# Linear attention and a gated FFN in one kernel: another written-out order, four output buffers, fewer matmuls on zeros

## The chip, the cores and the metric

The kernel runs on one core of a Trainium2 chip. The metric is the device time of one execution in microseconds. Before the change its median is 379.44 us over three runs (379.32 to 381.07).

## What is computed

Attention with an exponential feature map (batch 8, 8 heads, 576 tokens, head width 64, 128 features), then a gated FFN over the 4608 tokens of width 512:

```python
def phi(x):
    proj = np.einsum('bhsd,df->bhsf', x, w_phi)
    proj = proj - np.max(np.abs(proj), axis=-1, keepdims=True)
    return np.concatenate([np.exp(proj), np.exp(-proj)], axis=-1)
q_p, k_p = (phi(q), phi(k))
kv = np.einsum('bhsf,bhsd->bhfd', k_p, v)
z = np.sum(k_p, axis=2)
num = np.einsum('bhsf,bhfd->bhsd', q_p, kv)
den = np.einsum('bhsf,bhf->bhs', q_p, z)[..., None] + 1e-06
x = (num / den) ...                      # 4608 x 512
gate = np.maximum(x @ w_gate, 0.0)       # 512 -> 1536
return (gate * (x @ w_val)) @ w_out      # 1536 -> 512, float32
```

Everything is drawn and returned in float32; the kernel multiplies in bfloat16.

## The kernel before

The kernel is cut into 1430 small steps ("atoms", `Atoms`, L91), each a Python closure that issues a few instructions. The string ORDER lists their numbers; `Atoms.run` (L106) calls them in that order, and nothing else sets the order of the instructions on any engine. A number with an apostrophe calls the step's other variant: a PSUM copy goes to the other engine (ACT or DVE), a product of POOL to DVE. A word `zN` calls `keep_busy` (L196), which issues matmuls on a tile of zeros, two to a matmul of 128 x 512 and a single one as 128 x 256; their result is never read. Each engine works through its own instructions in the order in which they were issued, and waits at one whose inputs or buffers aren't ready.

The steps of one batch of keys ("items" of 4 to 8 blocks of 128 rows; `K_CUTS` cuts batch 0 into items of 4, 4, 8, 8, 8 and 4 blocks):

- load k and v. For batches 0 and 1, PE turns the blocks (L266) and DVE or ACT copies them out of PSUM (tile tT, L279); later batches are turned by a DMA on SP's queue (L291).
- project with w_phi (64-row matmuls, L307) into two PSUM banks; DVE takes the largest absolute value per row (tile mk, L314); ACT takes two exponentials per bank (tile kp, L363), and then the exponentials of the row maxima (tile ek, L374).
- scale v by them (tile vs, L323 on POOL; in the other variant a small ACT copy, L388, and DVE).
- 72 matmuls per half batch give kv (L447); ACT or DVE copies it (tile kv, L401).

For queries, in two pairs of chunks of 128 tokens per batch: turn (tile tT8 for batches 0 and 1), project both ways (L485 for the exponentials, L307 for the row maxima), two exponentials per bank on ACT (tile qp, L503), maxima on DVE (tile mq), their exponential on ACT (tile cq, L519); then matmuls with kv (L533), a product and a sum on DVE for each of three groups of heads (L552, L564), a reciprocal (L571) and the division on POOL (tile xu, L573), and the turn into xT (on PE for batches 0 and 1, L593; by DMA later).

The FFN (`ffn`, L652) runs in nine groups of 512 tokens: one per batch and a ninth for the batches' last 64 tokens each. A group has 12 value steps and 12 gate steps of four 128-row matmuls (L661); group 0 has 16, since its first 8 are only 256 tokens wide (`FIRST`). The value's copy goes to ACT or DVE (tile val_sb, L676), the gate's product is always DVE's (tile h, L683). Four output tiles of 12 matmuls follow (L709), each copied by ACT or DVE (L723) into an output buffer and stored by SP's queue. PSUM has eight banks, one pool for all.

The weights come in three thirds of w_val and w_gate and one load of w_out, all issued by POOL (L241, L250) between its other work, at the place that ORDER gives them. The transposing loads, the v loads and the stores are issued by SP, in their order too.

Of the kernel before, what the change touches and what calls it, by code (L numbers as in the profile page):

```python
# [8 lines left out]
FP32 = mybir.dt.float32  # L9
BF16 = mybir.dt.bfloat16  # L10
# [12 lines left out]

ORDER = """7 z6 49 50 59 60' z1 61 65 8 64 51 0 69 70' z1 71 1 62 66 67 68 z4 79 52 54 53 56 89 57 63 72 74 73
55 76 58 80 90 77 78 75 81 85 82 83 84 86 88 99 100' 91 92 94 z5 115 93 116 154 155 95 87 118 101
102 105 120 122 96 103 104 123 109 111' 124 128 10 127 126 110' 117 223 98 125 106 163 224 119 167
203 121 157 130 159 2 204 129 131 156 158 160 165 142 143 144 132 97 107 108 112 113' 4 114 161 193
z1 136 137 194' 29 45 133 134 162 166 138 135 148 149 3 139 145 146 9 150 147 151 233 168 187 181  # L30
184 185 182 188 164 234' 186 189 183 249 250' 190 205 140 141' 169 170 213 214' 152 153 175 209 176
288 289 207 172 173 177 174 171 178 1095 1096 1097 1098 1099 1100 208 1101 191 192' 179 180 195 199
1102 1103 196 13 206 235 237 198 239 1104 1105 1106 1107 1108 5 200 236 1109 1110 197 238 215 225
227 216 11 218 6 240 242 226 241 1111 1112 228 217 220 221 1113 252 291 254 256 293 1114 230 231'
219 1115 1116 210 229 1117 295 297 301 296 300 232 222 246 299 33 328 330 251 253 255 332 211 1118
247 248' 1119' 1120 201 298 258 290 292 262 202 260 294 212 243 257 244 245' 327 261 1121 1122 263
276 277 279 278 280 333 282 283 284 281 285 1123 1124 1125 309 302 310 329 303 304 1126 1127 318
319 320 259 321 322 306 307 1128 267 323 311 331 315 316 317 34 1129 1130 308 305 268 312 269 286
287 345 347 348 349 324 361 353 357 12 346 350 354 14 1131 1132' 355 363 264 1133 356 325 270 16
271 364 272 1134 326' 313 314' 1135 1136 265 266 273 362 366 367 365 358 360 337 338 339 1137 369  # L40
373 377 381 274 275 378 1138 370 371 372 374 380 351 379 1139' 1140 35 1141 352 391 395 36 359 433
437 375 397 435 1142 401 1143 399 368 340 341 334 342 1144 30 46 1145' 1146 393 1147 335 336 382
383 398 426 430 428 400 1148 1149 402 1150 384 432 434 376 17 427 431 429 436 385 387' 392 386 388
438 394 396 403 389 390' 461 463 477 480 19 1151 1152 410 481 411 462 1153 464 412 1154 1155 478 37
# [3 lines left out]
1168' 517 1169 485 488 486 495 474 548 552 508 512 497 468 510 490 498 499' 487 483 1170 18 1171'  # L48
550 1172 492' 1173 489 1174' 500 1175 1176 1177 1178 1179' 507 509 549 553 475 38 511 551 484 491
# [4 lines left out]
1198 676 678 680 603 606 627 1199 628 558 630 604 559 631 608 555 556 557 617' 632 602 541 629 1200  # L54
1201 1202 584 583 605 560 564 565 590 591 592 1203 1204 1205 1206 607 585 586 642 646 644 711 715
619 622 1207 587 588 589 623 620 593 624 626 712 714 713 1208 1209 21 1210 609 621 1211' 1212 1213'
1214 41 648 650 652 633 594 40 647 31 641 643 651 1215' 1216 1217' 649 1218 1219' 1220 645 682 686
610 684 677 634 679 635 637' 636 681 625 638 639 683 687 640 653 685 727 731 665 728 666 1221 1222
729 667 1223 730 657 658 659 688 47 716 26 1224 654 655 656 668 669 660 661 662 670 1225 1226 1227
717 671 672 673 1228 695 696 697 1229' 743 747 744 746 663 757 745 719 674 723 1230 720 1231 721  # L60
722 664 1232 703 704 1233' 1234 759 692 693 25 724 725 700 675 24 1235 726 689 732 705 701 718 702
748 1236 734' 694 706 707 708 690 691 698 1237 1238 793 795 799 761 797 798 699 800 733' 801 1239
802 1240 1241 735 739 709 758 710 737 762 760 764 766 749 738 736 740 768 750 344 769 803 1242 1243
1244 1245 1246' 792 796 828 741 832 804 830 751 794 827 753 742 754 755' 42 752 763 767 1247' 1248
756 787 788 781 782 789 765 833 783 43 32 1249' 1250 822 823 824 48 1251' 784 785 829 776 786 831
27 1252 777 790 1253 1254 773 774 845 846 775 861 863 791 847 778 1255 864 862 1256 1257' 770 771
865 849 772 779 808 809 1258 1259 840 810 1260 1261 819 841 842 1262 866 848 837 838 839 1263 1264
1265 1266 820 816 817 811 850 852 821 812 1267 1268 818 825 805 806 1269 1270 1271 853 813 807 780
867 897 899 855 856 869 870 872 1272 1273' 826 814 815 874 875 1274 1275 834 901 851 873 857 835
836 1276' 1277 1278 871 854 858 892 896 894 876 961 965 962 859 860 877 1279' 879 880 963 881 878  # L70
882 884 843 883' 1280 1281 1282 927 891 895 931 964 893 1283 929 1284 1285' 1286 1287' 932 934 898
900 936 902 903 1288 1289' 926 930 933 928 935 937 868 888 890 889 885 887 969 971 993 994 938 886'
977 970 996 995 979 1290 1291' 1292 1293 997 972 973 978 974 1294 1295' 981 921 922 923 1296 1297'
910 911 907 908 909 980 912 1298 1299 28 44 1300 1301 918 919 920 915 916 917 904 985 988 976 987
924 925 1007 1302 1303 986 1009 998 999 1304 1000 1011 950 951 982 983 905 906 844 953 1305' 1306
954 956 957 958 942 943 955 952 959 944 1307 1308 1309' 984 939 960 940 945 989 913 914 1310 1311
946 947 1014 1016 966 967 1018 1042 1046 941 948 990 1043 1047 1312 1313 949 1314 1315' 1045 1044
1316 1317 1318' 1013 1015 1017 1049 1051 968 975 1001 1002' 1003 991 992 1004 1005' 1006' 1048 1050
1008 1012 1319 1053 1054 1010 1019 1031 1032 1320 1321 1058 1322 1323' 1324 1033 1023 1325' 1052
1020 1069 1070 1326 1327 1061 1062 1063 1059 1060 1071 1328 1072 1329' 1037 1330 1073 1055 1056  # L80
1038 1039 1331 1332 1333 1334 1034 1035 1036 1021 1057 1064 1040 1024 1074 1335' 1336 1337 1338
1066 1067 1068 1339' 1340 1341 1342 1343 1026 1077 1079 1041 1065 1022 1078 1082 1075 1076 1344
1027 1028 1025 1029 1030 1081 1345' 1346 1347 1084 1080 1348 1349 1090 1350 1351' 1352 1083 1091
1087 1088 1092 1085 1086 1353 1354' 1355' 1356 1357' 1089 1358 1359' 1360 1361 1362 1363 1364 1365'
1366 1367' 1093 1094 1368 1369 1370 1371' 1372 1373' 1374 1375' 1376 1377 1378 1379 1380 1381' 1382
1383 1384 1385 1386 1387 1388 1389 1390 1391' 1392 1393' 1394 1395 1396 1397 1398 1399 1400 1401'
1402 1403 1404 1405' 1406 1407' 1408 1409 1410 1411' 1412 1413' 1414 1415 1416 1417' 1418 1419 1420
1421 1422 1423' 1424 1425 1426 1427 1428 1429'"""


class Atoms:  # L91
# [28 lines left out]
def kernel(  # L120
# [24 lines left out]
    DM = out.shape[1]  # L145
    P = 128
# [502 lines left out]
            q_tails(b // 2)  # L649


    def ffn(g):  # L652
        st = {}
        steps = [(fi, 0, SF) for fi in range(NFC)]
# [42 lines left out]

        for t in range(4):
            cols = LAST if g == B and t == 3 else ((0, DM),)
            for part, (c0, c1) in enumerate(cols):  # L700
                for third in range(3):

                    @atoms.add("fo", g, t, part, third)
                    def _(alt, t=t, part=part, third=third, c0=c0, c1=c1):
# [18 lines left out]
                        copy_by(copy_of(alt, "ACT", "DVE"))(out_sb, po)  # L723
                        store(t, out_sb, c0, c1)
# [55 lines left out]
```

## Time and profile before

| | us |
|---|---|
| median of three runs | 379.44 |
| the profiled execution | 381.42 |
| its span, first to last instruction | 379.6 |
| PE busy in the span | 368.2 |
| DVE busy | 288.1 |
| ACT busy | 218.0 |
| POOL busy | 136.2 |

A busy time is the union of an engine's instructions. The durations below come from the profiled execution, so sums are made against its 381.42 us, which is 2.0 us above the median.

### The profile page before, as it was taken

How to read it: one execution, taken by the hardware profiler on the slowest of the kernel's cores; microseconds unless marked ns; L12 is line 12 of the kernel's file. 1: busy time of each engine (PE TensorE's matmuls, PEld its weight loads, DVE VectorE, ACT ScalarE, POOL GpSimd, SP SyncE). 2: the span in 40 equal slices, each digit the busy share in tenths (PEclk: the TensorE clock that was granted, in tenths of full speed). 3: DMA queues.
4: the chain of work that ended last, by engine and by line, in shares of the span. 5: the costliest groups of instructions: out<-in, count | busy, mean ns of one | idle time of the engine just before them, and what ended most of it. 6: DMA issues, size and time to landing. Idle time of an engine off the chain costs nothing.

```text
span 379.6 us, 9748 instructions
## 1 busy us (share of the span) xinstructions
PE 368.2 (97%) x3891; PEld 196.7 (52%) x3891; DVE 288.1 (76%) x638; ACT 218.0 (57%) x538; POOL 136.2 (36%) x188
## 2 busy tenths in 40 slices
PE   6879999999999999999999999999999999999996
PEld 3557655546545555465555544545465454444443
DVE  2888988888986897889978987799677848723641
ACT  4978996988577867684776649766261221012101
POOL 5867451774247135441761137213810220100000
PEclk9989999999999999999999999999999999999999
DMA  8999997997969619793789503631400130011003
GB/s 254 205 195 195 208 173 92 241 226 103 153 202 240 119 29 166 218 172 52 138 225 149 152 2 111 98 46 28 120 36 2 29 112 28 16 51 59 2 2 109
DMA packets 75356, 45.15 MB, mean 119 GB/s; under 512 B 49392, under 2 KB 66352, under 8 KB 75312
## 3 DMA queue, kind: packets, MB, share of 16 engines
q1 hardware_dynamic: 53872, 30.42, 33.9%
q0 software_dynamic: 20960, 13.57, 26.2%
q8 instruction: 30, 0.49, 0.6%
q10 hardware_dynamic: 480, 0.56, 0.5%
q14 instruction: 14, 0.11, 0.1%
HBM read 37.78 MB, written 9.44 MB: 124 GB/s over the span
## 4 chain that ended last, share of the span: by engine, by line
PE 92%; ACT 6%; DMA 1%; issue 0%; SPq 0%; DVE 0%; DVEq 0%
PE pa L661 49%; PE pa L709 25%; PE pa L533 5%; PE pa L447 5%; PE pa L307 4%; ACT kp L363 3%; PE pa L485 2%; ACT qp L503 2%; PE pa L266 1%; DMA vn<-in_k_dram 1%; ACT tT L279 1%; ACT ek L374 0%; ACT xT L593 0%; SPq L218 0%; DVE u L723 0%
## 5 line engine op out<-in xcount | busy, mean ns | idle before, releaser
L661 PE MATMUL pa<-xT,wg_sb 128*128 128x512 bf16 (+1 forms) x400 | 99.3, 371 | 0.6 <-ACT val_sb L676 0.6
L709 PE MATMUL pa<-wo_sb,h 128*128 128x512 bf16 (+2 forms) x444 | 99.3, 373 | 0.0
L661 PE MATMUL pa<-xT,wv_sb 128*128 128x512 bf16 (+1 forms) x400 | 99.3, 370 | 0.0
L683 DVE SCALAR_TENSOR_TENSOR h<-pa,val_sb 128x512 bf16<-128x512 f32 (+1 forms) x112 | 74.5, 668 | 29.2 <-PE pa L661 21.8
L503 ACT ACTIVATE qp<-pa 128x512 bf16<-128x512 f32 x144 | 76.0, 613 | 25.2 <-PE pa L485 22.3
L573 POOL TENSOR_TENSOR xu<-u,r 128x512 bf16<-128x512 f32 x36 | 37.3, 1042 | 143.1 <-DVE r L571 111.3
L676 ACT CAST val_sb<-pa 128x512 bf16<-128x512 f32 (+1 forms) x70 | 39.7, 570 | 82.8 <-PE pa L661 78.1
L323 POOL TENSOR_TENSOR vs<-vn,ek 128x512 bf16<-128x512 f32 (+1 forms) x75 | 69.9, 945 | 41.9 <-ACT ek L374 33.5
L363 ACT ACTIVATE kp<-pa 128x512 bf16<-128x512 f32 (+1 forms) x164 | 79.0, 570 | 8.1 <-PE pa L307 6.9
L661 PEld LDWEIGHTS <-wv_sb 128*128 128x128 bf16 x448 | 41.7, 98 | 44.9 <-issue 1.1
L661 PEld LDWEIGHTS <-wg_sb 128*128 128x128 bf16 x448 | 41.4, 98 | 45.2 <-issue 1.5
L709 PEld LDWEIGHTS <-h 128*128 128x128 bf16 x444 | 40.9, 98 | 44.4 <-issue 0.3
L314 DVE TENSOR_REDUCE mk<-pa 128x4 f32<-128x512 f32 (+1 forms) x82 | 47.8, 616 | 6.5 <-ACT kp L363 4.2
L314 DVE TENSOR_REDUCE mq<-pa 128x4 f32<-128x512 f32 x72 | 46.6, 682 | 4.5 <-PE pa L307 4.4
L552 DVE TENSOR_TENSOR t<-pa,cq 128x195 f32<-128x195 f32 (+3 forms) x120 | 37.5, 328 | 4.3 <-PE pa L533 3.0
L564 DVE TENSOR_TENSOR u<-pa,t 128x195 f32<-128x195 f32 (+3 forms) x120 | 37.9, 333 | 2.9
L676 DVE CAST val_sb<-pa 128x512 bf16<-128x512 f32 x42 | 28.8, 686 | 11.0 <-PE pa L661 10.1
L533 PEld LDWEIGHTS <-qp 128*128 128x128 bf16 x640 | 28.8, 98 | 15.6 <-issue 0.8
L533 PE MATMUL pa<-kv,qp 128*128 128x65 bf16 x640 | 31.6, 194 | 0.5 <-ACT qp L503 0.5
L723 ACT COPY out_sb<-pa 128x512 f32<-128x512 f32 (+1 forms) x19 | 11.2, 590 | 30.4 <-PE pa L709 30.3
L723 DVE COPY out_sb<-pa 128x512 f32<-128x512 f32 x17 | 11.7, 689 | 17.0 <-PE pa L709 16.9
L447 PE MATMUL pa<-vs,kp 64*128 64x65 bf16 x1152 | 20.9, 193 | 0.5 <-ACT qp L503 0.4
(59 smaller groups left out, 229.1 us busy)
## 6 DMA issues: line engine op xcount, KB each, us to landing
out_dram<-out_sb SPq DMA_DIRECT2D x32, 256.0 KB, 2.4
vn<-in_v_dram SPq DMA_DIRECT2D x7, 1152.0 KB, 6.5
qn<-in_q_dram POOLq DMA_DIRECT2D x8, 512.0 KB, 7.3
kn<-in_k_dram POOLq DMA_DIRECT2D x7, 576.0 KB, 8.3
wv_sb<-in_moe_w_val_dram POOLq DMA_DIRECT2D x3, 512.0 KB, 8.2
wg_sb<-in_moe_w_gate_dram POOLq DMA_DIRECT2D x3, 512.0 KB, 9.5
wo_sb<-in_moe_w_out_dram POOLq DMA_DIRECT2D x1, 1536.0 KB, 20.7
vn<-in_v_dram SPq DMA_DIRECT2D x2, 288.0 KB, 4.9
```

The source lines that it names most:

```text
L314: nc.vector.tensor_reduce(m, some.rearrange("p (c f) -> p c f", f=F), axis=AX.X, op=ALU.max, apply_absolute_value=True,)
L323: eng.tensor_tensor(dst[:, :, s, 0:D], src, ek[:, :, s : s + 1].to_broadcast(list(src.shape)), op=ALU.mult,)
L363: nc.scalar.activation(st["kp"][:, s, 0 : n // 2, par, :], st["banks"][par][:, 0 : n // 2 * F].rearrange("p (a f) -> p a f", f=F), AF.Exp, ...
L447: nc.tensor.matmul(st["pk"][par][:, E * (2 * pair + s) : E * (2 * pair + s + 1)], lhsT=it["kp"][half_rows(par), s, c // 2, c % 2, :], rhs= ...
L503: nc.scalar.activation(x["qp"][:, s, slot].rearrange("p a b -> p (a b)"), st["cols", i][par], AF.Exp, scale=sign,)
L533: nc.tensor.matmul(pn[:, E * (2 * i + s) : E * (2 * i + s + 1)], lhsT=x["qp"][:, s, slot, blk, :], rhs=kv_of(b, lo + i)[:, s, :],)
L552: nc.vector.tensor_tensor(x["t", j][rows, 0:n], ab[:, :, 1], c[:, :, None].to_broadcast([np_, n, E]), op=ALU.mult,)
L564: nc.vector.tensor_tensor(x["u"][rows, lo : lo + n], ab[:, :, 0], x["t", j][rows, 0:n], op=ALU.add)
L661: nc.tensor.matmul(ps, lhsT=w[:, dc, P * fi : P * fi + P], rhs=xTs[g][:, dc, lo:hi], start=(dc == 0), stop=(dc == NDC - 1),)
L676: copy_by(copy_of(alt, "ACT", "DVE"))(st["val", n], ps)
L683: nc.vector.scalar_tensor_tensor(st["h2"][:, fi, lo:hi], ps, 0.0, st["val", n], op0=ALU.max, op1=ALU.mult)
L709: nc.tensor.matmul(po, lhsT=st["h2"][:, fi, P * t : P * t + P], rhs=wo_sb[:, fi, c0:c1], start=(fi == 0), stop=(fi == NFC - 1),)
```

## The change

Three things. ORDER is another string: up to the first loads of weights it is taken from an older kernel, and behind that it was made anew. Every step is still there once; the variants (apostrophes) are on 86 steps, where they were on 93. The words `zN` were z6, z1, z1, z4, z5, z1 (18 blocks, 11 matmuls) and are z6, z2, z2, z2 (12 blocks, 6 matmuls). And the output buffers are four: two of a pool of their own, and in turn with them the two tT8 buffers, which the queries of batches 0 and 1 use first.

```diff
-ORDER = """7 z6 49 50 59 60' z1 61 65 8 64 51 0 69 70' z1 71 1 62 66 67 68 z4 79 52 54 53 56 89 57 63 72 74 73
+ORDER = """7 z6 49 59 60' 50 51 53 61 63 55 8 64 1 52 0 69 70' z2 71 62 66 68 54 72 56 57' 58 z2 79 75 74 89
...
+    t_count = [0]
+
     def ffn(g):
...
+        def out_tile():
+            if t_count[0] % 2:
+                t = sb_g.tile([P, DM], FP32, name="out_sb", bufs=2)
+            else:
+                t = sb_T.tile([P, 8, P], BF16, name="tT8", bufs=2)
+                t = t.rearrange("p a b -> p (a b)").bitcast(FP32)
+            t_count[0] += 1
+            return t
...
-                            out_sb = sb_g.tile([P, DM], FP32, name="out_sb", bufs=3)
+                            out_sb = out_tile()
```

What the new order does to the start, at three places. In the rows below a tile's number is only a name; `x2` means two equal instructions in a row.

ACT from its first copy on, before (tT2_136 is item 1's turned blocks, kp_146 and kp_199 are the exponentials of items 1 and 0, ek the exponentials of their maxima):

```order
L279 CAST tT2_136<-pa_133 128x256
L363 ACTIVATE kp_146<-pa_141 128x2x128 x2
L279 CAST tT4_165<-pa_160 128x512
L374 ACTIVATE ek_181<-mk_151 128x4 x2
L363 ACTIVATE kp_199<-pa_153 128x2x128 x2
L374 ACTIVATE ek_202<-mk_196 128x4 x2
L363 ACTIVATE kp_146<-pa_140 128x2x128 x2
```

And ACT there now (tT2_134 is item 1's, kp_144 item 0's and kp_153 item 1's):

```order
L279 CAST tT2_134<-pa_131 128x256
L363 ACTIVATE kp_144<-pa_138 128x2x128 x2
L363 ACTIVATE kp_153<-pa_147 128x2x128 x2
L363 ACTIVATE kp_144<-pa_139 128x2x128 x2
L279 CAST tT4_171<-pa_166 128x512
L374 ACTIVATE ek_186<-mk_160 128x4 x2
L374 ACTIVATE ek_195<-mk_163 128x4 x2
L388 COPY pa_199<-ek_195 128x4
```

Item 0's exponentials moved ahead of item 1's, whose projection was the first on PE before and is now the second, and a small copy for a product of vs on DVE was added.

ACT around the kv copy of batch 0's second half (kv_612), before; cq_502 is the exponential of the first pair's maxima, qp_510 and qp_513 are the second pair's exponentials:

```order
L503 ACTIVATE qp_434<-pa_441 128x512 x2
L519 ACTIVATE cq_502<-mq16_332 128x16
L503 ACTIVATE qp_510<-pa_506 128x512 x2
L503 ACTIVATE qp_513<-pa_507 128x512 x2
L401 CAST kv_612<-pa_536 128x260
L279 COPY tT4_629<-pa_615 128x512
L503 ACTIVATE qp_513<-pa_646 128x512 x2
```

And ACT there now (kv_611 is the same copy, qp_418 and qp_318 are the first pair's two chunks, qp_534 and qp_658 the second pair's):

```order
L503 ACTIVATE qp_418<-pa_461 128x512 x2
L519 ACTIVATE cq_511<-mq16_334 128x16
L279 COPY tT4_514<-pa_497 128x512
L503 ACTIVATE qp_318<-pa_462 128x512 x2
L503 ACTIVATE qp_534<-pa_529 128x512 x2
L401 CAST kv_611<-pa_538 128x260
L519 ACTIVATE cq_621<-mq16_494 128x16
L503 ACTIVATE qp_658<-pa_528 128x512 x2
```

On PE that kv step stood behind products with both chunks of the first pair; now it stands behind those of one chunk, so that a copy and two pairs of exponentials are left to ACT beside it.

DVE at the first gate products of the FFN (h2), before; u_806 is the last chunk of attention output, tT8_793 turned q blocks of batch 1:

```order
L279 COPY tT8_793<-pa_784 128x1024
L552 TENSOR_TENSOR t_804<-pa_797,cq_685 128x195
L564 TENSOR_TENSOR u_806<-pa_774,t_782 128x130
L564 TENSOR_TENSOR u_806<-pa_797,t_804 128x195
L564 TENSOR_TENSOR u_806<-pa_752,t_759 128x195
L571 RECIPROCAL r_810<-u_806 128x8
L683 SCALAR_TENSOR_TENSOR h2_821<-pa_822,val_sb_819 128x256
L683 SCALAR_TENSOR_TENSOR h2_821<-pa_835,val_sb_833 128x256
L683 SCALAR_TENSOR_TENSOR h2_821<-pa_848,val_sb_846 128x256
L314 TENSOR_REDUCE mk_854<-pa_736 128x4
```

And DVE there now (u_811 is the last chunk; the changed kernel's L685 and L678 are L683 and L676 of before):

```order
L564 TENSOR_TENSOR u_811<-pa_786,t_806 128x195
L564 TENSOR_TENSOR u_811<-pa_779,t_784 128x130
L564 TENSOR_TENSOR u_811<-pa_766,t_804 128x195
L571 RECIPROCAL r_815<-u_811 128x8
L685 SCALAR_TENSOR_TENSOR h2_819<-pa_820,val_sb_798 128x256
L685 SCALAR_TENSOR_TENSOR h2_819<-pa_833,val_sb_831 128x256
L678 CAST val_sb_844<-pa_839 128x256
L685 SCALAR_TENSOR_TENSOR h2_819<-pa_855,val_sb_844 128x256
L314 TENSOR_REDUCE mk_873<-pa_672 128x4
```

The copy of turned q blocks went to ACT, and a copy of the value came to DVE.

More of the change, by code (lines that the diff above doesn't have):

```diff
@@ L31 @@
[L31 to L41, printed above, removed]
@@ L55 @@
[L55 to L65, printed above, removed]
@@ L66 @@
[L66 to L83, printed above, removed]
@@ new lines @@
+67' 80 65 81 84 73 76 90' 91 94 83 82 99 85 77 z2 115 86 95 154 92 100' 101 116 93 155 104 123 78
+127 96 118 122 88 120 87 109 102 10 125 110 233 234 111 106 124 103 126 203 204 223 224 117 2 157
+105 128 98 119 163 165 167 213 107 130 129 97 214' 159 108 131 29 45 121 156 132 160 112 114 142
+161 168 113' 143 144 162 9 148 149 145 146 133 158 3 150 147 136 137 205 5 151 134 164 172 169 138
+166 135 139 175 176 177 173 193 194' 152 153' 288 4 170 174 171 249 140 141 184 289' 250' 11 187
+188 181 1095 178 185 182 207 183 189 186 190 1096 1097 1098 1099' 209 6 179 180' 1100 1101 191 208
@@ new lines @@
+539 582 1186 534 535 536 614 572 22 569 573 1187 570 571 574 602 613 1188 1189 612 579 530 1190 21
+566 567 1191 568 531 532 47 575 561 562 533 1192 1193 1194 1195' 563 1196 615 558 559 560 1197 1198
+627 616 603 583 631 604 605 540 541 676 680 1199 628 630 555 576 606 556 1200 1201 1202 618 632 557
+617 564 565 633 634 590 591 1203 584 592 608 585 586 1204' 1205 1206 607 678 629 619 622 642 644
+646 711 343 712 621 1207 715 1208 1209 620 714 623 587 588 589 713 610 624 1210 1211' 1212 593 594
@@ new lines @@
+1077 1037 1038 1337' 1076 1338 1039 1040 1041 1339 1340 1081 1341 1020 1021 1022 1028 1342 1343
+1083 1029 1030 1344 1079 1084 1345' 1346 1347 1348 1090 1349 1087 1350 1351' 1352 1088 1353 1089
+1085 1086 1091 1092 1093 1354' 1355 1094 1356 1357' 1358 1359' 1360 1361' 1362 1363' 1364 1365 1366
+1367' 1368 1369 1370 1371' 1372 1373' 1374 1375' 1376 1377' 1378 1379 1380 1381 1382 1383 1384 1385
+1386 1387 1388 1389 1390 1391 1392 1393' 1394 1395' 1396 1397 1398 1399 1400 1401' 1402 1403 1404
+1405 1406 1407' 1408 1409' 1410 1411' 1412 1413' 1414 1415 1416 1417 1418 1419 1420 1421 1422 1423'
@@ L91 @@
+1424 1425 1426 1427 1428 1429'"""
 class Atoms:
```

37 lines of the change are left out of this document (22 added, 15 removed), and 29 rows, old and new, of the table ORDER.

## The prediction

> **What bounds the kernel now.** I read the busy time by stretch first. Its columns are the stretch, its length, then busy time of PE, PEld, DVE, ACT and POOL with instruction counts, the granted clock, the DMA share and GB/s.
>
> ```profile
> 0.00:20.00 20.00, 14.62 (x176) 8.87 (x177) 11.99 (x25) 14.97 (x45) 14.62 (x29) 1.00 1.06 229
> 20.00:40.00 20.00, 17.71 (x280) 14.24 (x280) 16.80 (x50) 16.38 (x41) 12.49 (x16) 0.91 1.14 197
> 40.00:60.00 20.00, 20.00 (x294) 10.84 (x292) 17.20 (x34) 17.58 (x47) 9.02 (x14) 1.00 1.34 188
> 100.00:200.00 100.00, 100.00 (x1210) 52.74 (x1207) 84.80 (x193) 69.81 (x179) 45.36 (x61) 1.00 0.76 155
> 300.00:376.00 76.00, 75.90 (x402) 35.74 (x400) 39.07 (x69) 11.41 (x21) 3.12 (x3) 1.00 0.15 46
> ```
>
> From 40 us to the last matmul PE is never idle, at full clock. Before that it is idle for 5.4 us of the first 20 and 2.3 us of the next 20, and a clock of 0.91 takes more. So the kernel is a start of some 35 us that other engines set, followed by a queue of PE work. An order that starts the queue 1 us earlier ends 1 us earlier; one that only shuffles the queue ends at the same time, as long as nothing runs dry.
>
> The chain that ended last says who sets the start (begin, length, engine, line):
>
> ```profile
> 5.52 0.38 ACT tT L279
> ...
> 22.32 1.09 ACT qp L503 x2
> ...
> 23.46 2.13 PE pa L447 x71
> ...
> 33.65 0.27 ACT val_sb L676
> ...
> 33.97 1.91 PE pa L661 x16
> ...
> 48.93 1.10 PE pa L447 x72
> ```
>
> ACT owns it almost without a break from 5.52 to 23.4 us and from 27.29 to 33.9; only the piece between lies on PE, beginning with the kv step (L447) at half clock: 71 matmuls in 2.13 us, where 72 later take 1.10. At 33.97 the second gate step of the first FFN starts and PE hardly stops again.
>
> **The change, term by term, up to that point.** In the timeline (begin, length, engine, instruction, in brackets the idle time ahead of it and who ended it) four places of the start are touched:
>
> ```profile
> 5.52 0.37 ACT L279 CAST tT<-pa 128x256 bf16<-128x256 f32 x1 [2.17 <-PE pa L266]
> 6.39 0.66 ACT L363 ACTIVATE kp<-pa 128x256 bf16<-128x256 f32 x2 [0.49 <-PE pa L307]
> 25.64 0.38 ACT L401 CAST kv<-pa 128x260 bf16<-128x260 f32 x1 [1.25 <-PE pa L447]
> 27.29 1.08 ACT L503 ACTIVATE qp<-pa 128x512 bf16<-128x512 f32 x2 [0.53 <-PE pa L485]
> 33.95 0.42 DVE L683 SCALAR_TENSOR_TENSOR h<-pa,val_sb 128x256 bf16<-128x256 f32 x1
> ```
>
> *Start of ACT.* Before, the first exponentials wait for the projection of item 1, whose transposed copy ACT makes itself (5.52 to 5.89). Now the projection of item 0 stands first on PE; its copy is DVE's and is ready long before. ACT can go on at 5.9 instead of 6.39: **-0.5 us**.
>
> *ACT's idle time around kv.* Before, ACT has nothing to do for 1.25 us ahead of the kv copy and 0.53 us a little later. Now two pairs of q exponentials and a 128x512 copy stand between the first chunk's exponential and that kv copy; 2.07 us (four exponentials, row below) and 0.58 us of work cover the 1.1 to 2.1 us of kv. So ACT gains up to **-1.8 us** here.
>
> *Work that moves between ACT and DVE.* Counting the orders up to the first FFN copy (ACT) and the first gate product (DVE): ACT has four fewer 128x512 exponentials, one more CAST of 128x512, one more COPY of 128x1024, one fewer of 128x256, two more kv casts and two small copies for vs. DVE loses a CAST of 128x512, a COPY of 128x1024 and two kv casts, and takes a 128x256 copy and two vs products.
>
> ```profile
> 31.58 2.07 ACT L363 ACTIVATE kp<-pa 128x512 bf16<-128x512 f32 x4
> L279 ACT CAST tT<-pa 128x512 bf16<-128x512 f32 x1 | 0.6, 585 | 0.6 <-PE pa L266 0.6
> L279 ACT COPY tT<-pa 128x1024 bf16<-128x1024 bf16 x1 | 1.1, 1060 | 0.0
> L279 ACT COPY tT<-pa 128x256 bf16<-128x256 bf16 x1 | 0.4, 395 | 0.0
> L401 ACT CAST kv<-pa 128x260 bf16<-128x260 f32 x17 | 6.3, 401 | 1.6 <-PE pa L447 1.6
> L388 ACT COPY pa<-ek 128x4 f32<-128x4 f32 x2 | 0.3, 165 | 0.0
> L279 DVE CAST tT<-pa 128x512 bf16<-128x512 f32 x2 | 1.4, 693 | 0.7 <-PE pa L266 0.7
> L279 DVE COPY tT<-pa 128x1024 bf16<-128x1024 bf16 x3 | 2.0, 685 | 0.0
> L401 DVE CAST kv<-pa 128x260 bf16<-128x260 f32 x15 | 6.3, 423 | 3.7 <-PE pa L447 3.7
> L323 DVE TENSOR_TENSOR vs<-vn,pa 128x256 bf16<-128x256 f32 x2 | 0.8, 416 | 0.5 <-ACT pa L388 0.5
> ```
>
> ACT: -2.07 + 0.58 + 1.06 - 0.40 + 0.80 + 0.33 = **+0.3 us**. DVE, with 0.4 us taken for the 128x256 copy that it doesn't show: -0.69 - 0.69 - 0.85 + 0.4 + 0.83 = **-1.0 us**.
>
> *Which of them decides.* ACT alone would come to the first FFN copy at -0.5 - 1.8 + 0.3 = -2.0 us. But that copy feeds a gate product on DVE, which is queued behind the 24 products and sums of the attention output. Their long run starts when the kv copy is done: walking ACT's new queue with the durations above I get there about 0.5 us earlier. The DVE work behind that point is one COPY of 128x1024 shorter (0.7). So the first gate product moves from 33.95 by -0.5 - 0.7 = **-1.2 us**; ACT's other 0.8 us is lost in waiting for DVE.
>
> *Between the first gate product and a full PE.* The exponentials and maxima of batch 1 that ACT and DVE had done before (four exponentials, 2.07 us) now stand among the first FFN steps, and one projection more is issued ahead of the gate step 3, so that its two PSUM banks are held. Between nothing (the FFN copies of steps 2, 4, 5, 8 and 9 go to DVE and relieve ACT) and the whole 2.07 us I take **+0.4**, near the lower end, because DVE arrives with less behind it.
>
> *Zeros.* Seven wide and four half-wide matmuls become six wide ones.
>
> ```profile
> L200 PE MATMUL pa<-zeros 128*128 128x512 bf16 x7 | 3.1, 555 | 1.0 <-DVE zeros L742 1.0
> ```
>
> Three wide ones less are at most 1.7 us at 0.555 us each. They all lie in the first 27 us, where PE waits for ACT anyway: **0**, unless the clock answers; that is the second rival.
>
> *Loads.* POOL issues the weights' loads between its other work. The first two change places, both far ahead of the first FFN step; the last third of w_val is now issued behind the second attention output on POOL, near 31 us by my walk, and is first read in step 12, some 18 us later. At 9.5 us to landing (row below) nothing waits: **0**; if it landed late, PE would stand still in step 12 by as much.
>
> *After 40 us.* The order is another one, but the PE work is the same: 224 FFN half-steps, 36 output tiles, 16 kv steps. What an order can still cost PE is the change between 64-row matmuls (kv and the projections) and 128-row ones, since the weight load that opens such a run isn't hidden: "PEld L307" below waits 12 times, 4.9 us together, for nothing but itself. From step 8 of the first FFN on both orders have 62 such changes: **0**. The output buffers, four for three, remove no wait, since the copies into them (L723) waited for PE only.
>
> ```profile
> wg_sb<-in_moe_w_gate_dram POOLq DMA_DIRECT2D x3, 512.0 KB, 9.5
> PEld L307 <- issue: 4.9, 12, 0.4
> ACT out_sb L723 <- PE pa L709: 30.3, 10, 8.9
> out_dram<-out_sb SPq DMA_DIRECT2D x32, 256.0 KB, 2.4
> ```
>
> A store lands 2.4 us after its issue, so a buffer is soon free. The two borrowed ones are last read by PE, in the projections of batch 1's q (L307), which stand some 4 us of PE work ahead of the first output tile in PE's own order. If that order were turned round, an output copy would wait for them, and PE for its bank.
>
> **Sum.** -1.2 + 0.4 = -0.8 us. The profiled execution took 381.42 us (span 379.6), 2.0 more than the median of 379.44; it would become 380.6, and the median **378.6 us**. The bounds: ACT's full -2.0 with nothing given back, and -1.2 + 2.07 = +0.9.
>
> **The clock, rule and row.** The granted clock around the half-speed piece:
>
> ```profile
> 16.50:20.00 3.50, 2.69 (x88) 1.91 (x87) 3.50 (x9) 3.50 (x13) 3.46 (x6) 1.00 1.25 210
> 20.00:23.40 3.40, 2.51 (x35) 1.43 (x35) 2.99 (x8) 3.38 (x11) 3.40 (x6) 1.00 1.36 180
> 23.40:26.80 3.40, 3.34 (x86) 3.11 (x85) 2.27 (x7) 1.95 (x5) 1.54 (x3) 0.50 1.24 204
> 26.80:30.20 3.40, 2.92 (x58) 2.18 (x56) 3.16 (x15) 2.91 (x7) 2.04 (x2) 1.00 1.53 193
> ```
>
> After a stretch with PE busy 2.51 of 3.40 us the clock fell to half for one stretch of 3.4 us, then rose again. After 2.69 of 3.50 it stayed. The Trainium skill, page "TensorE: Matmul & The Clock Gate", Part 1, states that half rate is the default, that a busy window of about 3.4 us lifts it and an idle one brings it back, which speaks against taking zeros away. The length of the stretch agrees with it; the trace differs in that the window ahead was far from idle. By the rule a thinner PE stays at half clock longer, and that is the second rival.
>
> **Rivals.**
> 1. *Everything on ACT arrives.* DVE finds its inputs early and nothing is given back: -2.0 us, 377.4. For it: ACT owns the chain for most of the start. Against: DVE was busy 3.16 of the 3.40 us from 26.8 on. Chance 0.25, with some room below.
> 2. *The clock.* With fewer zeros and longer waits PE drops to half in one or two more stretches. As long as they lie ahead of 27 us ACT covers most of it; from the point where the FFN starts, every stretch costs half its length, 1.7 us. One of them early (kv again at 2.13 for 1.10, +1.0) and one in the FFN (+1.7), on top of the forecast: 381.3; two in the FFN: 382.0. It decides if PE's busy share in a stretch from about 27 us on falls to that of 20.00:23.40. Slower than before; chance 0.15.
> 3. *PE runs dry later.* The new order from 40 us on isn't covered as well as the old: a load of v or a transpose stands too close ahead of its first reader on the queue of SP, or DVE (84.8 of 100 us busy) gets its work in lumps. Each idle microsecond of PE is one in the result. In the new order the v load of batch 2 stands only some 4 us of PE work ahead of its first product on POOL, but the kv step that needs it comes 19 us later. A few such places give +2 to +3: 381 to 382. Chance 0.12.
>
> Forecast: the remaining 0.48. **Range:** 376.9 (the first rival with 0.5 to spare) to 382.0. About 0.5% (1.9 us) is what a measurement of this kernel can tell from no change. Below 377.5 lie most of the first rival and a little of the forecast, 0.27; above 381.3 most of the second and third and a little of the forecast, 0.23; between them 0.50.
>
> **What would show it.** Right: ACT's first exponential near 5.9 us, no idle ACT of more than 0.5 us ahead of the kv copy, the first gate product near 32.8 us on DVE, and PE full from 40 us on as before. Wrong: a granted clock under 1 in a stretch after 27 us; gaps on PE after 40 us; or a first gate product at 34 us or later, which would mean that DVE or a wait for a PSUM bank, and not ACT, set the start.

## The result, and the profile after

The change made the kernel slower: **382.26 us** median of 22 runs (377.92 to 383.71) against 380.19 of 22 runs before (379.16 to 381.67), a ratio of **1.0042** (95% interval 1.0023 to 1.0060). The ratio leaves out two of the changed kernel's runs as slow (383.61 and 383.71) and isn't the quotient of the two medians, which is 1.0054. The forecast was 378.6 with a range from 376.9 to 382.0. The profiled execution took 382.97 us, its span is 381.2.

The busy time by stretch of the changed kernel (columns as in the prediction):

```profile
0.00:20.00 20.00, 13.90 (x187) 8.60 (x188) 12.74 (x27) 16.08 (x51) 14.04 (x28) 1.00 1.06 230
20.00:40.00 20.00, 18.65 (x302) 14.39 (x298) 18.34 (x53) 18.59 (x42) 11.04 (x14) 1.00 1.30 201
40.00:60.00 20.00, 16.52 (x185) 8.17 (x180) 11.64 (x22) 11.57 (x32) 10.89 (x16) 0.91 1.20 190
60.00:100.00 40.00, 40.00 (x569) 22.50 (x562) 36.90 (x85) 33.66 (x81) 17.90 (x24) 1.00 0.88 160
```

The second row is better than before (PE 18.65 for 17.71, clock 1.00 for 0.91). The third is the new one: between 40 and 60 us, where PE had been busy 20.00 of 20 us, it is idle for 3.5, and the clock is 0.91 there, that is, half for some 3.4 us, worth up to another 1.7. From 60 us on PE is full again. So the loss is in one place.

The start, in the timeline of ACT and then of DVE (begin, length, engine, instruction, in brackets idle time ahead and its ender):

```profile
5.24 0.37 ACT L279 CAST tT<-pa 128x256 bf16<-128x256 f32 x1 [1.77 <-PE pa L266]
5.57 1.76 ACT L363 ACTIVATE kp<-pa 128x256 bf16<-128x256 f32 x6
23.51 0.53 ACT L401 CAST kv<-pa 128x260 bf16<-128x260 f32 x1
```
```profile
31.43 0.39 DVE L685 SCALAR_TENSOR_TENSOR h<-pa,val_sb 128x256 bf16<-128x256 f32 x1
```

The three marks that the prediction named for the start are there (the fourth, a full PE from 40 us on, isn't): the first exponential directly behind ACT's first copy, no idle time ahead of the kv copy (1.25 us before), and the first gate product early, at 31.43 where 33.95 was and 32.8 was forecast.

The waits between 40 and 56 us, largest first (who waited, for whom; total, times, longest):

```profile
POOL vs L323 <- ACT val_sb L678: 10.7, 1, 10.7
DVE mq L314 <- PE pa L307: 4.5, 1, 4.5
PEld L447 <- issue: 3.7, 2, 3.2
PE pa L447 <- POOL vs L323: 3.5, 2, 3.0
```

PE stands for 3.5 us in the kv step of batch 1 (L447) for products that POOL makes (vs, L323), and POOL had itself stood for 10.7 us. The engine named there, ACT, can't be the cause: its copy val_sb feeds no product of vs. POOL's timeline and PE's show the order of events:

```profile
44.36 1.04 POOL L323 TENSOR_TENSOR vs<-vn,ek 128x512 bf16<-128x512 f32 x1 [10.69 <-ACT val_sb L678]
...
46.45 2.19 POOL L323 TENSOR_TENSOR vs<-vn,ek 128x512 bf16<-128x512 f32 x3
...
48.74 1.04 POOL L323 TENSOR_TENSOR vs<-vn,ek 128x512 bf16<-128x512 f32 x1
...
49.88 2.05 POOL L323 TENSOR_TENSOR vs<-vn,ek 128x512 bf16<-128x512 f32 x2
```
```profile
47.56 0.36 PE L447 MATMUL pa<-vs,kp 64*128 64x65 bf16 x12 [0.44 <-POOL vs L323]
50.97 1.19 PE L447 MATMUL pa<-vs,kp 64*128 64x65 bf16 x60 [3.05 <-POOL vs L323]
```

The first product starts at 44.36 us and the sixth ends near 51; PE waits for it. What starts the first one is its other input, vn, the v load of batch 1. The rows are its issue on SP's queue and its time from issue to landing, of after:

```profile
29.80 0.43 SPq L218 DMA_DIRECT2D vn<-in_v_dram  x1
```
```profile
vn<-in_v_dram SPq DMA_DIRECT2D x1, 1152.0 KB, 14.4
```

And of before:

```profile
33.46 0.39 SPq L218 DMA_DIRECT2D vn<-in_v_dram  x1
```
```profile
vn<-in_v_dram SPq DMA_DIRECT2D x1, 1152.0 KB, 5.5
```

29.80 + 14.4 = 44.2, 0.2 us ahead of POOL's first product. The load is issued 3.7 us earlier than before and lands 5.2 us later (33.46 + 5.5 = 39.0). What stands around it are POOL's loads of weights and k, first of after, then of before:

```profile
22.83 1.55 POOL L241 DMA_DIRECT2D wg_sb<-in_moe_w_gate_dram  x2
28.16 0.81 POOL L241 DMA_DIRECT2D wv_sb<-in_moe_w_val_dram  x1
28.95 0.76 POOL L218 DMA_DIRECT2D kn<-in_k_dram  x1
32.58 1.09 POOL L250 DMA_DIRECT2D wo_sb<-in_moe_w_out_dram  x1
```
```profile
24.16 0.79 POOL L241 DMA_DIRECT2D wg_sb<-in_moe_w_gate_dram  x1
34.93 0.96 POOL L212 DMA_DIRECT2D qn<-in_q_dram  x1
35.88 0.77 POOL L241 DMA_DIRECT2D wg_sb<-in_moe_w_gate_dram  x1
36.63 0.77 POOL L218 DMA_DIRECT2D kn<-in_k_dram  x1
37.36 1.06 POOL L250 DMA_DIRECT2D wo_sb<-in_moe_w_out_dram  x1
```

Before, POOL issued nothing between 24.9 and 34.9 us, so the v load at 33.46 had the DMA engines nearly to itself: between 34 and 38 us no packet of POOL's queue moves. Now two loads are queued just ahead of it, the thirds issued at 22.83 may still run, and w_out (1536 KB) 2.8 us behind it.

The packets in the traces show where the v load's 8.9 us more (14.4 for 5.5) are lost. Ahead of it on SP's own queue stands qmT, the transposing load of the last 64 tokens of q, with 512 packets of 256 bytes; the v load is 512 packets of 2304 bytes. The time to landing of qmT, of after and of before:

```profile
qmT<-qm SPq DMA_TRANSPOSE x1, 9.2
```
```profile
qmT<-qm SPq DMA_TRANSPOSE x1, 3.5
```

In before qmT's packets move from 32.2 to 33.6 us and the v load's from 34.5 to 38.5. In after qmT's move from 31.4 to 36.9, among those of POOL's loads, and the v load's only from 36.4 to 43.7. So some 5.5 us of the 8.9 pass before its first packet (6.6 us behind its issue, in before 1.0), and some 3.3 while it moves itself. The packets of POOL's queue (q0) and SP's (q1), their MB and share, of after from 34 to 36 us and from 38 to 40, and of before from 36 to 38:

```profile
q0 software_dynamic: 315, 0.31, 91.8%
q1 hardware_dynamic: 314, 0.08, 29.9%
```
```profile
q0 software_dynamic: 174, 0.20, 57.6%
q1 hardware_dynamic: 169, 0.39, 56.0%
```
```profile
q1 hardware_dynamic: 330, 0.76, 103.0%
```

Where both queues have work, they move about the same number of packets, small or large. So POOL's loads cost the v load time twice, by way of qmT and by sharing with it.

### The profile page after: what moved, and what is told of

It reads as the page before. It is cut to its first block, busy times and chain, and to the rows that moved or that the text cites. A ratio compares the mean times of both kernels' runs of the same rounds, so it can differ in the third digit from the quotient of the medians.

```text
span 381.2 us, 9742 instructions
## 1 busy us (share of the span) xinstructions
PE 366.5 (96%) x3886; PEld 195.4 (51%) x3886; DVE 281.2 (74%) x629; ACT 225.1 (59%) x550; POOL 135.8 (36%) x186
## 4 chain that ended last, share of the span: by engine, by line
PE 88%; ACT 6%; POOL 1%; DVE 1%; DMA 1%; issue 1%; SPq 0%; DVEq 0%; POOLq 0%; ACTq 0%
PE pa L663 48%; PE pa L720 25%; PE pa L533 5%; PE pa L307 4%; PE pa L447 4%; ACT kp L363 2%; PE pa L485 2%; ACT qp L503 2%; POOL vs L323 1%; ACT tT L279 1%; DMA vn<-in_k_dram 1%; DVE mk L314 1%; PE pa L266 1%; ACT ek L374 0%; DVE h L685 0%
## 5 line engine op out<-in xcount | busy, mean ns | idle before, releaser
L685 DVE SCALAR_TENSOR_TENSOR h<-pa,val_sb 128x512 bf16<-128x512 f32 (+1 forms) x112 | 74.6, 669 | 42.6 <-PE pa L663 31.7
L503 ACT ACTIVATE qp<-pa 128x512 bf16<-128x512 f32 x144 | 77.0, 621 | 14.5 <-PE pa L485 14.4
L678 ACT CAST val_sb<-pa 128x512 bf16<-128x512 f32 (+1 forms) x77 | 44.4, 582 | 69.5 <-PE pa L663 64.5
L323 POOL TENSOR_TENSOR vs<-vn,ek 128x512 bf16<-128x512 f32 (+1 forms) x74 | 69.3, 948 | 34.7 <-ACT ek L374 13.6
L663 PEld LDWEIGHTS <-wv_sb 128*128 128x128 bf16 x448 | 41.9, 98 | 45.5 <-issue 2.6
L533 PE MATMUL pa<-kv,qp 128*128 128x65 bf16 x640 | 31.4, 193 | 0.8 <-ACT qp L503 0.5
L678 DVE CAST val_sb<-pa 128x512 bf16<-128x512 f32 (+1 forms) x35 | 23.3, 665 | 3.7 <-PE pa L663 2.8
L447 PE MATMUL pa<-vs,kp 64*128 64x65 bf16 x1152 | 20.3, 190 | 3.7 <-POOL vs L323 3.5
L734 ACT COPY tT<-pa 128x512 f32<-128x512 f32 x11 | 6.4, 585 | 28.6 <-PE pa L720 28.5
L447 PEld LDWEIGHTS <-kp 64*128 64x128 bf16 x1152 | 19.1, 94 | 4.5 <-issue 4.3
```

Source lines behind the costliest of these rows:

```text
L323: eng.tensor_tensor(dst[:, :, s, 0:D], src, ek[:, :, s : s + 1].to_broadcast(list(src.shape)), op=ALU.mult,)
L447: nc.tensor.matmul(st["pk"][par][:, E * (2 * pair + s) : E * (2 * pair + s + 1)], lhsT=it["kp"][half_rows(par), s, c // 2, c % 2, :], rhs= ...
L503: nc.scalar.activation(x["qp"][:, s, slot].rearrange("p a b -> p (a b)"), st["cols", i][par], AF.Exp, scale=sign,)
L533: nc.tensor.matmul(pn[:, E * (2 * i + s) : E * (2 * i + s + 1)], lhsT=x["qp"][:, s, slot, blk, :], rhs=kv_of(b, lo + i)[:, s, :],)
L663: nc.tensor.matmul(ps, lhsT=w[:, dc, P * fi : P * fi + P], rhs=xTs[g][:, dc, lo:hi], start=(dc == 0), stop=(dc == NDC - 1),)
L678: copy_by(copy_of(alt, "ACT", "DVE"))(st["val", n], ps)
```

## The experiments

Three explanations were set against each other: **L**, the v load of batch 1 lands late because POOL's loads share the DMA engines with it and with what stands ahead of it on SP's queue; **P**, POOL has too many products of vs in a row ahead of that kv step; **Z**, fewer zeros cost clock. The early gain was then taken apart in the same way. Each ratio is to runs of before on the same chip:

| kernel | us (runs) | ratio to before (95%) | v load 1 to landing, us |
|---|---|---|---|
| after | 382.26 (22) | 1.0042 (1.0023 to 1.0060) | 14.4 |
| e1_v1_clear | **377.18** (6) | 0.9923 (0.9903 to 0.9943) | 7.2 |
| e2_before_v1_crowded | 382.05 (12) | 1.0059 (1.0029 to 1.0088) | 11.9 |
| e3_vs_split | 384.03 (6) | 1.0095 (1.0058 to 1.0132) | 14.0 |
| e4_zeros_back | 381.99 (12) | 1.0041 (1.0024 to 1.0058) | 14.1 |
| e5_v1_early | 377.63 (6) | 0.9936 (0.9921 to 0.9952) | 10.9, issued over 16 us earlier |
| e6_k2_wo_later | 379.79 (12) | 1.0004 (0.9981 to 1.0027) | 12.1 |
| e10_wg2_later | 379.40 (12) | 0.9989 (0.9969 to 1.0009) | 12.3 |
| e7_three_buffers | 377.14 (4) | 0.9923 (0.9911 to 0.9936) | 7.6 |
| e8_start_of_before | 377.18 (4) | 0.9923 (0.9910 to 0.9935) | 7.6 |
| e9_before_to_ffn | 379.93 (12) | 0.9983 (0.9967 to 1.0000) | 5.6 |
| e11_kv_behind_n | 378.23 (12) | 0.9947 (0.9932 to 0.9962) | 7.6 |

Lines of the experiments made from after are one lower than in after (L322 for L323 and so on), since ORDER takes a line less. A profile is one execution, and those of e4 and e11 are the fastest of their 12 runs.

### e1_v1_clear: the loads around the v load moved away

In ORDER, 5 and 4 are the last thirds of w_gate and w_val, 11 is k of batch 2, 6 is w_out, 190 the last attention output of batch 0 on POOL.

```diff
-137 205 5 151 134
+137 205 4 151 134
...
-153' 288 4 170 174
+153' 288 170 174
...
-289' 250' 11 187 188
+289' 250' 187 188
...
-186 190 1096 1097
+186 190 5 11 6 1096 1097
...
-1099' 209 6 179 180'
+1099' 209 179 180'
```

> The changed kernel with four loads moved on POOL's queue: the last third of w_val takes the place of the last third of w_gate, and that one, k of batch 2 and w_out are issued behind the last attention output of batch 0 (near 32.6 us) instead of up to 4 us ahead of the v load of batch 1 or right behind it. Theory L (the v load of batch 1, 14.4 us to landing where it took 5.5, makes POOL and then the kv step of batch 1 late): it lands in about 9 us, near 39, POOL starts its products at 39 to 40, the gap of PE at 47 to 53 us and the half clock behind it go, and the time falls by 4 to 5.4 us, to 377 to 378, under the kernel before. Theory P (it is POOL's chain of six products ahead of that kv step, whenever it starts): the gap stays at 3 us or more, 380 to 381. Theory Z (fewer zeros bring the clock down): 382, with a half-clock stretch somewhere before 60 us.

The v load was issued at 29.73 (29.80 in after), took half as long, with qmT ahead of it landing in 5.7 us for 9.2, and POOL's first product came 6.8 us earlier; now it waits for its own exponentials:

```profile
vn<-in_v_dram SPq DMA_DIRECT2D x1, 1152.0 KB, 7.2
```
```profile
37.53 1.04 POOL L322 TENSOR_TENSOR vs<-vn,ek 128x512 bf16<-128x512 f32 x1 [2.73 <-ACT ek L373]
```

The stall is gone, and with it 5.1 us: 377.18, 0.77% under before. L stands, and this is a version that beats both kernels.

### e2_before_v1_crowded: the crowd brought into before

```diff
-149 3 139 145
+149 3 5 139 145
...
-250' 190 205 140
+250' 190 11 6 205 140
...
-1107 1108 5 200 236
+1107 1108 200 236
...
-227 216 11 218 6 240 242
+227 216 218 240 242
```

> The kernel before with the reverse: the last third of w_gate is issued right behind the middle third (near 25 us), k of batch 2 and w_out ahead of the last attention output of batch 0 (near 32 us), so that all stand ahead of the v load of batch 1 (33.5 us). Theory L: that load takes 10 to 15 us instead of 5.5, lands at 44 to 48, and PE gets a gap at the kv step of batch 1 (near 50 us): 2 to 5 us slower than before. Theories P and Z: no change within 0.5 us, since POOL's products and the zeros are those of before.

The load took 11.9 us instead of 5.5, and the median rose by 1.9 us. The runs fell into two groups, six from 380.19 to 381.05 and six from 383.06 to 386.72; the profiled execution, 381.05, belongs to the lower and shows only 0.7 us of waiting for POOL in the kv step of batch 1. The granted clock is alike in both groups (0.991 to 0.996 in the lower, 0.990 to 0.996 in the upper), so the upper group's loss isn't the clock. The direction is that of L, but what the upper group paid for wasn't seen. Before's own order needs the load later than after's, as POOL's first product in before shows:

```profile
43.32 0.61 POOL L323 TENSOR_TENSOR vs<-vn,ek 128x256 bf16<-128x256 f32 x1 [4.91 <-ACT ek L374]
```

It waits for its exponentials until 4.3 us after the load's landing at 39.0, so a load landing at 43.8 (31.91 + 11.9, e2) is nearly in time: POOL's first product starts at 44.00 there, 0.7 us later.

### e3_vs_split: two of the products to DVE

```diff
-1112 13 221 235 236
+1112 13 221' 235 236
...
-298 210 232 231 246
+298 210 232' 231 246
```

> The changed kernel with two of the six products of POOL that stand ahead of the kv step of batch 1 given to DVE (the other variant of the steps vs 1.2.0 and vs 1.3.1, each with small ACT copies). Theory P: POOL's chain is 2.1 to 2.3 us shorter, the kv step ends that much earlier, -2.1 us, and -3.8 if the clock then stays up: 378.5 to 380. Theory L alone, with the landing at 44 us as the only cause: no more than -1, since all six products wait for it anyway and DVE's two wait as well. Theory Z: nothing, 382.

The median rose by 1.8 us more, though the intervals of e3 and after overlap by a little. DVE now stands at the same load, and everything behind it on DVE too; the waits between 40 and 56 us:

```profile
POOL vs L322 <- DMA vn<-in_v_dram: 10.6, 1, 10.6
...
ACT kp L362 <- DVE mk L313: 4.3, 1, 4.3
DVE vs L322 <- DMA vn<-in_v_dram: 3.3, 1, 3.3
PE pa L662 <- DVE vs L322: 3.0, 1, 3.0
```

Here the view itself names the load. A shorter chain of products on POOL gained nothing, which speaks against P; as DVE now waits too, e3 alone can't rule it out. e5 does: it leaves POOL's work as it is.

### e4_zeros_back: the zeros of before

```diff
-51 53 61 63
+51 53 z1 61 63
...
-69 70' z2 71 62
+69 70' z1 71 62
...
-57' 58 z2 79 75
+57' 58 z4 79 75
...
-85 77 z2 115 86
+85 77 z5 115 86
...
-173 193 194' 152
+173 193 z1 194' 152
```

> The changed kernel with the number of matmuls on zeros of before (z6, z1, z1, z4, z5, z1, at the same neighbours). Theory Z: PE warms up sooner and stays up, -1.5 to -2 us, 380.5. Theories L and P: within 0.5 us of the changed kernel, 382.3, with the same gap at 47 to 53 us, since the first 45 us of the changed kernel already ran at full clock from 10.9 us on and gained 2.5 us on before.

No difference to after (1.0041 for 1.0042). The stall is there (PE waits 3.0 us for POOL in L446, the load took 14.1). Z has fallen. The profiled execution is the fastest of the 12, 380.32 us; its clock stayed at 1.00 through the stall, so it shows the stall without the half clock: 3.1 us over e1.

### e5_v1_early: the load itself given out earlier

9 is the v load of batch 1; 29 and 45 are the load of the last 64 tokens of q and its turn, which SP waits for.

```diff
-108 131 29 45
+108 131 9 29 45
...
-144 162 9 148 149
+144 162 148 149
```

> The changed kernel with one step moved: the v load of batch 1 is given to SP's queue ahead of the turn of the last 64 tokens (which SP issues at 28.26 us because it waits for their load), so that it can be issued near 4 us, right behind the loads of batch 0. Nothing is moved on POOL's queue, the five loads of POOL between 21.4 and 32.6 us stay. Theory L (the load lands too late for batch 1's kv step, because it shares the DMA engines with POOL's loads): it lands before 20 us, POOL's first product of batch 1 no longer waits 10.7 us, the stall of PE at 45 to 55 us (5.4 us lost) is gone, and the time is 3.5 to 5.4 us below that of the changed kernel, 377 to 379, less up to 2 us if 1.15 MB more in the first 15 us delay q, k and the first thirds of the weights. Rival (the stall belongs to the order of the work and not to the load: POOL has too many products ahead of the kv step): POOL's first product starts earlier but the gap of PE at 45 to 55 us keeps more than 3 us, 381 to 383.

377.63. SP issues the load within its first 14 us, POOL's loads stay crowded, and the stall is gone all the same. So it is the landing that counts. By this place the load passes SP's turn, which waited for its own load until 28.26 us in after, and whose packets then held the v load back. POOL's work is the same and the stall is gone, so P has fallen. Other loads pay a little (w_gate's first third takes 15.3 us to landing, where it took 11.5 in after) without a loss that shows.

### e6_k2_wo_later and e10_wg2_later: the halves of e1

e6 moves only k of batch 2 and w_out. e10 moves only the two thirds: 4 takes the place of 5, as in e1, and 5 alone is put behind 190.

```diff
-289' 250' 11 187 188
+289' 250' 187 188
...
-186 190 1096 1097
+186 190 11 6 1096 1097
...
-1099' 209 6 179 180'
+1099' 209 179 180'
```

> The changed kernel with two loads moved: k of batch 2 and w_out are issued behind the last attention output of batch 0 on POOL, instead of at 28.95 and 32.58 us; the last thirds of w_gate and w_val stay where the changed kernel has them (22.83 and 28.16 us). It tells which neighbours the v load of batch 1 shares the DMA engines with. If w_out and k2, which are queued while it runs, are what stretches it: it takes 7 to 9 us to landing in place of 14.4, the stall is gone or under 1 us, 377 to 379. If the two thirds issued ahead of it are what holds it: 12 us or more to landing, a stall of 2 us or more stays, 380 to 382.

> The changed kernel with the last third of w_val in the place of the last third of w_gate (near 23 us), and that third issued behind the last attention output of batch 0 on POOL; k of batch 2 and w_out stay as in the changed kernel, at 28.95 and near 32.6 us. It is the other half of e1_v1_clear beside e6_k2_wo_later (12.1 us to landing of the v load of batch 1, where both halves together gave 7.2 and neither 14.4). If what is issued ahead of the v load counts most: 8 to 10 us to landing, no stall, 377 to 378.5. If only the bytes queued count, wherever they stand: 12 us or more, a stall of 1 us or more, 379 to 381.

Each half gives about a half (0.38% and 0.53% of the 1.19% between after and e1). POOL's first product of batch 1, of e6 and of e10:

```profile
42.33 1.05 POOL L322 TENSOR_TENSOR vs<-vn,ek 128x512 bf16<-128x512 f32 x1 [8.07 <-DMA vn<-in_v_dram]
```
```profile
42.08 1.05 POOL L322 TENSOR_TENSOR vs<-vn,ek 128x512 bf16<-128x512 f32 x1 [8.04 <-DMA vn<-in_v_dram]
```

And the wait of PE for it, the same row in both:

```profile
PE pa L446 <- POOL vs L322: 1.8, 1, 1.8
```

e10 came out as expected for the case that only the queued bytes count (12.3 us to landing). It doesn't settle that, though: with w_val's third gone, k of batch 2 still stood 1.8 us ahead of the v load. qmT took 7.9 (e6) and 8.4 us (e10) to land, between e1's 5.7 and after's 9.2. Landing at 42.1 (e6) and 41.9 (e10) costs PE 1.8 us, at 44.2 (after) 3.5, at 36.9 (e1) nothing: from these, estimated, about 40 us is where the delay begins to show.

### e7_three_buffers and e8_start_of_before: two parts worth nothing

e7 is e1 with three buffers of one pool:

```diff
-                            out_sb = out_tile()
+                            out_sb = sb_g.tile([P, DM], FP32, name="out_sb", bufs=3)
```

> The kernel of e1_v1_clear (377.18 us) with three output buffers of a pool of their own, as before the change, in place of two of their own and two borrowed ones. If the buffers are worth nothing, as the prediction has it (the output copies wait for PE only, a store lands 2.4 us after its issue): 377.2 within 0.4. If the fourth buffer carries a part of the time: 378 or more.

377.14: the fourth buffer is worth nothing. In e8 the first 72 entries are before's, zeros included, and the rest follows in e1's order:

```diff
-7 z6 49 59 60' 50 51 53 61 63 55 8 64 1 52 0 69 70' z2 71 62
+7 z6 49 50 59 60' z1 61 65 8 64 51 0 69 70' z1 71 1 62 66 67
...
```

> The kernel of e1_v1_clear (377.18 us) with the start of before: the steps up to the first kv step (its first 72 entries, five words of zeros among them) stand as before the change has them, everything behind as in e1_v1_clear. It tells how much of the early gain (2.5 us of PE's lost time up to 45 us) the older kernel's start brought. By the prediction's terms the start is worth 0.5 us by ACT and the rest lies behind it: 377.2 to 377.9, first exponential of ACT near 6.4 us and first gate product near 32 us. Rival (the start carries the gain): 378.5 to 379.7, first gate product of DVE at 33 us or later.

377.18, the same as e1. Its first exponential is again late behind ACT's first copy, and its first gate product isn't:

```profile
4.33 0.37 ACT L278 CAST tT<-pa 128x256 bf16<-128x256 f32 x1 [0.79 <-PE pa L265]
5.20 0.66 ACT L362 ACTIVATE kp<-pa 128x256 bf16<-128x256 f32 x2 [0.49 <-PE pa L306]
```
```profile
30.98 0.39 DVE L684 SCALAR_TENSOR_TENSOR h<-pa,val_sb 128x256 bf16<-128x256 f32 x1
```

### e9_before_to_ffn and e11_kv_behind_n: where the early gain comes from

e9 has before's first 174 entries, up to the first FFN step, and behind them e1's order. e11 is e1 with one entry moved (112 and 114 are the kv step and a copy, 142 the products with kv of the first pair's second chunk):

```diff
-132 160 112 114 142 161 168
+132 160 142 112 114 161 168
```

> The kernel of e1_v1_clear (377.18 us) with everything of before up to the first FFN step (its first 174 entries: batch 0's attention, the first projections of batch 1, the loads and the zeros among them); from there on the changed kernel's order, with the last third of w_gate, k of batch 2 and w_out as the first loads behind that point. e8_start_of_before showed that the first 72 entries are worth nothing. If the gain of 3 us comes from the order between the first kv step and the FFN (the prediction's idle time of ACT around the kv copy, and what it frees on DVE): 379.0 to 380.3, ACT idle for 1.2 to 1.3 us ahead of its kv copy, and the first gate product of DVE about 28.4 us behind ACT's first copy as in before (33.95 less 5.52). If it comes from the FFN steps and batch 1's work among them: 377.2 to 378, whatever the kv copy does.

> The kernel of e1_v1_clear (377.18 us) with one step moved: the second half of batch 0's kv step on PE stands behind the products with kv of the first pair's second chunk (as in before) instead of ahead of them. It tests the prediction's largest term by itself. If the position of that step is what ended ACT's idle time ahead of the kv copy: 0.5 to 1.3 us of idle time come back there, and 377.6 to 378.5. If ACT's other work covers it anyway, or DVE sets the pace there: 377.2 within 0.3.

ACT at its kv copy, of e9 and of e11:

```profile
24.74 0.38 ACT L400 CAST kv<-pa 128x260 bf16<-128x260 f32 x1 [1.25 <-PE pa L446]
```
```profile
23.70 0.38 ACT L400 CAST kv<-pa 128x260 bf16<-128x260 f32 x1 [0.68 <-PE pa L446]
```

Both ratios lie above e8's by more than the half-widths of e8's interval: e9 by 0.60% of 380.2, **2.3 us**, e11 by 0.24%, **0.9 us** (e11's interval and e8's still overlap by 0.03%). With the idle time the first gate product comes back late in e9, at 33.27 us; in e11 it stands at 31.46, 0.4 behind e1's 31.08. So the gain lies between the first kv step and the FFN, and the place of the kv step on PE is about a third of it, the less certain part.

Not all of e9's 2.3 us is waiting. Its profile has a granted clock of 0.83 between 20 and 40 us, where e1 and e8 have 1.00, and its 71 matmuls of the kv step take 2.13 us, as in before, for 1.42 (72 matmuls) in after. Its three runs at a clock of 1.0 took 378.26 to 378.75 us, 1.1 to 1.6 over e8; the other nine ran at 0.991 to 0.995. So, estimated, about half of the 2.3 us goes with the clock.

## Why the prediction was wrong

- **Loads: 0. This step failed.** It asked of the thirds that it saw move whether they land ahead of their own reader, and took the landing time of before (9.5 us for a third) as fixed (w_val's last third, expected near 31 us, was issued at 28.16, ahead of the v load). It named neither w_gate's last third nor k of batch 2 nor w_out as moved, and never asked what POOL's loads do to the loads of SP. There qmT's 3.5 us to landing became 9.2, the 5.5 of the v load behind it 14.4, and the lost time (3.5 us of waiting, up to 1.7 of half clock) is the 4.5 to 5.1 us that e1 takes away again (1.0042 - 0.9923 = 1.2% of 380.2, or the difference of the medians).
- **After 40 us: 0** failed with it. The statement that PE work is the same was true, the statement that nothing runs dry was not. The third rival had the mechanism in words, a load of v too close ahead of its first reader, but looked at batch 2, by PE work between the places in ORDER. Batch 1's load was issued 3.7 us *earlier*; only its time to landing shows the danger.
- *Start of ACT, -0.5.* Seen in the trace at the right size (the first exponential 0.33 us behind the start of ACT's first copy for 0.87), and worth nothing: e8 undoes it, with the rest of the first 72 entries, without a loss. What absorbs it wasn't seen.
- *ACT's idle time around kv, and DVE.* Right in kind: the idle time went, and e9 and e11 bring it back with a loss. Of the size, taken together -1.2 us by the first gate product, no more than this is shown: measured from ACT's first copy, that product moved from 28.43 (33.95 - 5.52) to 26.19 (31.43 - 5.24) in after, by -2.2 us, and to 26.70 in e1, whose start is the same, by -1.7. Part of that is the kv step at full clock, 1.42 us for 2.13, which the sum left out. Whether DVE set the pace, as the prediction had it, stays open.
- *Between the first gate product and a full PE, +0.4.* Little was given back: PE is busy 18.65 of the 20 us to 40, and in e1 it is busy 19.84 of the next 20 and 39.58 of the 40 behind them, 0.6 us less than in before. The first rival's 377.4 is what e1 came to, 377.18, without the load's stall.
- *Zeros 0, buffers 0.* Right: e4 and e7.

The sum as measured: -2.9 (1 - 0.9923 of 380.2) for the order of the start, and +4.5 to +5.1 for the load, give +1.6 to +2.2; the ratio says +1.6, the medians +2.1. Open are the three of after's 22 runs at 377.92 to 379.11. Their granted clock is 0.998 to 1.0, that of the other 19 runs 0.989 to 0.996. A clock that stayed up isn't enough to explain them, since e4's execution at 1.0 kept the stall and took 380.32; they would fit a v load that landed in time, but none of them has a trace.

## What to carry to other kernels

When an order moves loads, list the loads that *weren't* moved, and ask of each what shares the DMA engines with it and what stands ahead of it on its own queue; a landing time belongs to its neighbours as much as to its size (here 5.5 of the 8.9 us were lost on the load ahead of it, 3.3 on its own transfer), and a median over seven loads hides the one that is late. When a wait is put down to an engine that can't feed the instruction, look for the DMA: here the load's issue plus its landing time met the end of the wait within 0.2 us. A late input is mended at the load (other places for its neighbours, or an earlier issue past a waiting instruction on its queue), not by giving its readers to another engine, which then waits as well.

## What the runs showed of the hardware

- One load of 1152 KB on SP's queue took 5.5, 7.2, 12.1 and 14.4 us to landing, by what POOL's queue had to move at the same time. The Trainium skill, page "DMA: Bandwidth & Descriptors", section "Queues, rings and completion order", says that each DMA engine goes round the queues that have work, a packet at a time. The trace agrees: 315 packets of POOL's queue and 314 of SP's from 34 to 36 us, 174 and 169 from 38 to 40. By this the v load moved 0.39 MB in 2 us beside POOL's packets, where before it moved 0.76 alone, and qmT with its 256-byte packets moved 0.08. Within SP's queue the v load stood behind qmT: in after its first packet moved at 36.4 us, shortly before qmT's last at 36.9.
- The clock. PE's stretches around the stall, of after and then of e4, which has the same stall:

```profile
48.00:51.81 3.81, 0.84 (x56) 0.84 (x57) 0.54 (x1) 1.35 (x5) 3.81 (x7) 1.00 1.30 181
51.81:55.23 3.42, 3.42 (x33) 1.58 (x26) 1.92 (x4) 1.99 (x5) 3.42 (x6) 0.50 1.43 157
```
```profile
48.00:51.81 3.81, 1.85 (x71) 1.46 (x72) 0.33 (x1) 1.30 (x4) 3.81 (x6) 1.00 1.27 189
51.81:55.23 3.42, 3.39 (x16) 1.57 (x16) 2.59 (x5) 2.30 (x7) 2.43 (x4) 1.00 1.43 178
```

  A stretch busy 0.84 of 3.81 us was followed by one at half clock, one busy 1.85 of 3.81 was not, though before had fallen after 2.51 of 3.40. The busy share of a stretch cut by hand doesn't foretell it.
- The start of an execution varies by about a microsecond. POOL's wait for the first k load, of before and of e8, which has the same first steps:

```profile
4.80 0.19 POOL L747 COPY gate<-vn 128x1 f32<-128x1 f32 x1 [3.14 <-DMA vn<-in_k_dram]
```
```profile
3.61 0.19 POOL L757 COPY gate<-vn 128x1 f32<-128x1 f32 x1 [1.95 <-DMA vn<-in_k_dram]
```

  Before's profiled execution (381.42 us) lies 1.2 above the median of 22 runs; the late first load is as much, though that it is the reason isn't shown. Marks of two profiles agree to about half a microsecond, from either zero: after and e1, whose start is the same order, have their first gate product at 31.43 and 31.08 from the span's start, and at 26.19 and 26.70 from ACT's first copy.
